# A gated recurrence and an FFT convolution in one kernel: the hidden state kept in natural order, and its transposes as float32r matmuls on an identity

## The chip, the cores and the metric

One core of a Trainium2 chip runs the whole program. The metric is device time in microseconds (us). TensorE is written PE (its weight loads PEld), VectorE is DVE, ScalarE is ACT, GpSimd is POOL, SyncE is SP; SP issues all DMAs of this kernel. SBUF is the on-chip memory with 128 partitions, PSUM the eight banks (512 float32 per partition each) that PE writes.

## The reference, cut to what matters

```
# x, f_logit: [4, 6272, 256] float32; lower_bound: [256]
f = lower_bound + (1 - lower_bound) * sigmoid(f_logit)
i = 1 - f
for t in range(6272):                      # for each batch and channel
    h = f[:, t] * h + i[:, t] * x[:, t]
    y[:, t] = h
proj = y @ w_proj                          # w_proj: [256, 768]
x1, x2, x3 = proj split in three
x2_conv = irfft(rfft(x2, time) * rfft(filter_fft, time))   # circular, length 6272
out = (x1 * x2_conv * x3) @ w_out          # [4, 6272, 256] float32
```

The length is 6272 = 128 x 49. The kernel computes the circular convolution as a two-dimensional transform over these factors, all as matmuls on small constant matrices.

## The kernel before, in words

Everything is done batch by batch (four batches, `b` = 0 to 3), and inside a batch in stages. Python generators hold the stages, and `weave` calls two of them alternately, so that their instructions are emitted in turn; a scheduler of the language then settles the order on each engine, and each engine works through its own list in order.

- `hgrn(b)` is the recurrence. It goes over time in 16 chunks of 392. SP loads a chunk of x (`xt`) and of f_logit (`ft`) with time on the partitions, 98 rows to a block. ACT takes the sigmoid, POOL multiplies (line 123), PE transposes both into PSUM (`sT` line 128, `uT` line 132) so that the channels lie on the partitions; ACT makes the gate `fT` (line 135), DVE runs the scan (line 138). The two halves of the channels (`kh` = 0, 1) do this one after the other. POOL then copies the scan's float32 result to float16 into `hG` (line 143), where times with the same remainder modulo 49 lie together.
- `phase_p(b)` projects h to x2. For each of 49 values of `q` POOL copies a rotated piece of `hG` into `hP` (lines 364 and 366), PE multiplies (line 368), ACT casts the result (line 370). `phase_f1(b)` is the first transform (PE line 382) and DVE and ACT in turn write its result `A` (lines 386, 388).
- `phase_z(b)` makes the gates x1 and x3 (16 matmuls of 512 columns for a group, line 406), ACT scales one (line 411), DVE multiplies the two into `z` (line 412).
- `units(b)` has 16 steps: PE transforms `A` (`px`, line 442), DVE multiplies by the filter's spectrum (lines 446 and 447), combines real and imaginary parts into `Y` (lines 450, 451), POOL adds a column (line 452), PE transforms back (`pi`, lines 457 and 459), ACT writes `Th` (line 463). `mini(b)` does the same for a special frequency.
- `phase_o(b)` finishes: PE (`pc`, line 478), DVE multiplies into `z` (line 482), PE multiplies by w_out (`po`, line 491), ACT scales (line 495), SP writes the output.
- `prepare` computes the constants and the filter's spectrum once: seven loads of 896 KB (line 287), a float32 matmul that rotates the rows (line 293), a split into two float16 parts (ACT line 297, DVE line 298), then 16 steps of transforms (lines 306 to 308 and 324).

The order of the stages is: `hgrn(0)` woven with `prepare`; then for each batch `phase_p` and `phase_f1` woven with `phase_z`, then `mini`, then `units` woven with the next batch's `hgrn`, then `phase_o`. PSUM tiles come from pools: two buffers for the transposes (`pst`), one for `px` (`psx`), two for all else (`psm`).

## Time and profile before

| what | value |
|---|---|
| two timed runs | 1226.43 and 1230.41 us, median 1228.42 us |
| the profiled execution | 1228.79 us; its span 1227.1 us; mean granted PE clock 0.803 |
| busy, share of the span | PE 73%, PEld 47%, DVE 52%, ACT 41%, POOL 32% |
| moved by DMA | 85.50 MB, mean 70 GB/s |

The span reaches from the first to the last instruction; what lies around it is 1.7 us. No engine is busy all the time, so the table alone does not name a bound: each stage has its own. The profile's groups give the mean time of one instruction and what ended the engine's waits; its windows give the busy time of each engine, and the clock that PE was granted, by stage.

### The profile page before, as it was taken

To read this page: it belongs to the slowest core of one execution; us is meant where nothing else is said; L and a number is where in the kernel's file an instruction comes from. 1 tells how busy PE (TensorE), PEld (TensorE's weight loads), DVE (VectorE), ACT (ScalarE), POOL (GpSimd) and SP (SyncE) were. 2 spreads that over 40 slices of the span, in tenths; PEclk is the share of its full clock that TensorE was granted. 3 is DMA by queue.
4 is the path that set the end of the run, shared out by engine and by line. 5 is a ranking of instruction groups with operands and counts; after the bars stand their busy time and mean duration, and the time that the engine had idled before them with its cause. 6 is when DMAs were issued, how large, how long until landed. Compare 5 with 4: busy or idle time off the path is not lost.

```text
span 1227.1 us, 14846 instructions
## 1 busy us (share of the span) xinstructions
PE 892.4 (73%) x5784; PEld 577.3 (47%) x5784; DVE 639.7 (52%) x806; ACT 504.3 (41%) x649; POOL 386.8 (32%) x701
## 2 busy tenths in 40 slices
PE   2676789886678848776778677867788568767765
PEld 1444566443355536543455455434455454333344
DVE  7766743123579834223779632235898322346632
ACT  5676754463233324543333324633333226321122
POOL 5433441450136593000346761001465800000000
PEclk9996599999955569999755579998655799995579
DMA  6344411000023425100233334000233130000013
GB/s 199 97 124 122 122 56 51 28 1 1 2 78 105 114 78 190 65 1 1 53 82 111 97 123 168 1 1 26 68 106 91 52 141 19 1 1 0 1 69 142
DMA packets 61350, 85.50 MB, mean 70 GB/s; under 512 B 3040, under 2 KB 53984, under 8 KB 61280
## 3 DMA queue, kind: packets, MB, share of 16 engines
q1 hardware_dynamic: 61280, 84.55, 21.9%
q8 instruction: 45, 0.74, 0.3%
q14 instruction: 25, 0.20, 0.1%
HBM read 58.85 MB, written 25.69 MB: 69 GB/s over the span
## 4 chain that ended last, share of the span: by engine, by line
PE 46%; DVE 28%; POOL 9%; ACT 8%; issue 7%; DMA 3%; POOLq 0%; SPq 0%; DVEq 0%; ACTq 0%
PE p L406 15%; PE po L491 8%; PE px L442 5%; DVE z L482 4%; DVE p L446 4%; DVE z L412 4%; DVE Y L451 4%; ACT x1s L411 4%; PE pfx L324 3%; PE pr L293 3%; DVE A L386 3%; DVE h L138 3%; POOL hP L366 3%; POOL xt L123 3%; PE pc L478 2%
## 5 line engine op out<-in xcount | busy, mean ns | idle before, releaser
L143 POOL CAST hG<-h 128x392 f16<-128x392 f32 x128 | 109.6, 861 | 359.9 <-PE p L406 262.2
L406 PE MATMUL p<-hG,W13h 128*128 128x512 f16 (+1 forms) x416 | 150.3, 368 | 83.2 <-DVE z L412 42.5
L123 POOL TENSOR_TENSOR xt<-xt,ft 98x1024 f32<-98x1024 f32 x64 | 157.4, 2461 | 131.5 <-DMA xt<-in_x_dram 54.9
L412 DVE TENSOR_TENSOR z<-p,x1s 128x512 f16<-128x512 f32 (+1 forms) x104 | 68.4, 658 | 182.4 <-ACT x1s L411 182.4
L463 ACT CAST Th<-pi 128x784 f16<-128x784 f32 x64 | 52.0, 812 | 245.9 <-PE pi L459 245.9
L406 PE MATMUL p<-hG,W13l 128*128 128x512 f16 (+1 forms) x416 | 150.3, 367 | 0.0
L132 PE MATMUL uT<-iden,xt 98*128 98x98 f32 x512 | 107.2, 353 | 53.5 <-ACT fT L135 27.9
L482 DVE TENSOR_TENSOR z<-pc,z 128x1024 f16<-128x1024 f32 (+1 forms) x52 | 60.5, 1163 | 153.7 <-PE pc L478 153.7
L491 PE MATMUL po<-Woh,z 128*128 128x256 f16 x392 | 99.3, 294 | 55.1 <-DVE z L482 53.2
L442 PE MATMUL px<-A,FT 98*128 98x512 f16 x256 | 118.9, 593 | 27.0 <-DVE p L447 20.4
L411 ACT ACTIVATE x1s<-p 128x512 f32<-128x512 f32 (+1 forms) x104 | 59.5, 572 | 169.1 <-PE p L406 168.6
L138 DVE TENSOR_TENSOR_SCAN h<-fT,h,uT 128x392 f32<-128x392 f32 x120 | 120.6, 1024 | 11.2 <-PE uT L132 7.1
L132 PEld LDWEIGHTS uT<-iden,xt 98*128 98x128 f32 x512 | 80.0, 206 | 85.1 <-ACT fT L135 43.5
L128 PE MATMUL sT<-iden,ft 98*128 98x98 f32 x512 | 105.3, 352 | 19.4 <-ACT ft L122 16.0
L457 PE MATMUL pi<-VA,Y 98*128 98x196 f16 x256 | 84.4, 364 | 43.9 <-POOL Y L452 43.9
L491 PEld LDWEIGHTS <-z 128*128 128x128 f16 x784 | 77.9, 105 | 77.1 <-DVE z L482 62.2
L446 DVE TENSOR_TENSOR p<-px,H 98x1024 f16<-98x1024 f32 x64 | 78.2, 1222 | 64.0 <-PE px L442 64.0
L128 PEld LDWEIGHTS sT<-iden,ft 98*128 98x128 f32 x512 | 83.2, 210 | 45.2 <-issue 14.9
L495 ACT ACTIVATE osb<-po 128x1024 f32<-128x1024 f32 (+1 forms) x52 | 50.6, 974 | 129.0 <-PE po L491 122.4
L406 PEld LDWEIGHTS <-W13l 128*128 128x128 f16 x416 | 40.5, 97 | 131.5 <-issue 97.1
L135 ACT ACTIVATE fT<-sT,nomc 128x392 f32<-128x392 f32 x128 | 77.4, 605 | 53.7 <-PE sT L128 51.4
L491 PE MATMUL po<-Wol,z 128*128 128x256 f16 x392 | 98.6, 292 | 0.0
(129 smaller groups left out, 1522.4 us busy)
## 6 DMA issues: line engine op xcount, KB each, us to landing
xt<-in_x_dram SPq DMA_DIRECT2D x64, 392.0 KB
ft<-in_f_logit_dram SPq DMA_DIRECT2D x64, 392.0 KB
out_dram<-osb SPq DMA_DIRECT2D x48, 512.0 KB
fraw<-in_moe_filter_fft_dram SPq DMA_DIRECT2D x7, 896.0 KB
wp<-in_moe_w_proj_dram SPq DMA_DIRECT2D x1, 768.0 KB
out_dram<-osb SPq DMA_DIRECT2D x4, 128.0 KB
wo<-in_moe_w_out_dram SPq DMA_DIRECT2D x1, 256.0 KB
wcol<-in_lower_bound_dram SPq DMA_DIRECT2D x1, 1.0 KB
```

The costliest lines, as they stand in the source:

```text
L123: nc.gpsimd.tensor_tensor(xt[:TB], xt[:TB], ft[:TB], op=AOP.mult)
L128: nc.tensor.transpose(sT[:, j * TB:(j + 1) * TB], ft[:TB, j, cols], iden[:TB, :TB])
L132: nc.tensor.transpose(uT[:, j * TB:(j + 1) * TB], xt[:TB, j, cols], iden[:TB, :TB])
L138: nc.vector.tensor_tensor_scan(h32[:], fT[:], uT[:, 0:CH], 0.0 if last[kh] is None else last[kh][:, CH - 1:CH], op0=AOP.mult, op1=AOP.add)
L143: nc.gpsimd.tensor_copy(hG[b][:, kh, :, c * MR:(c + 1) * MR], h32[:].rearrange("p (m r) -> p r m", r=Q))
L406: nc.tensor.matmul(p13[:, i, 0:cn], w[:, kh, js], hG[b][:, kh, r0:r0 + rn, :], start=(n == 0), stop=(n == 3))
L411: nc.scalar.activation(x1s[:, 0:cn], p13[:, 0, 0:cn], AF.Copy, scale=ZS)
L412: nc.vector.tensor_tensor(z[:, jb, r0:r0 + rn, :], p13[:, 1, 0:cn], x1s[:, 0:cn], op=AOP.mult)
L442: nc.tensor.matmul(px[:, o, :], FT[:TB, tb, :], A[:TB, es, r, :], start=(n == 0), stop=(n == 1))
L446: nc.vector.tensor_tensor(p0[:TB], px[:TB], H[:TB, :, u, :], op=AOP.mult)
L482: nc.vector.tensor_tensor(zz, pc[:, :, 0:rn * 128].rearrange("p a (i m) -> p a i m", m=128), zz, op=AOP.mult)
L491: nc.tensor.matmul(po[:, i, :], z[:, kh, r0 + i, :], w[:, kh, :], start=(n == 0), stop=(n == 3))
```

## The change

The hidden state is kept in the order of time, in float16, in one long tile `HA`: half 0 at the start, half 1 at the end, and between them the room of 16384 columns that holds `A`. The scan writes straight into it. What `phase_p` needs from `h` modulo 49 is read by PE with a step of 49 columns as the stationary operand; because such a read runs over the end of time, six DMAs (`wraps`) copy each half once more into the room of `A`, after `A` has been used. `phase_z` reads 490 consecutive columns (10 groups of 49) as its moving operand, and its DVE multiply brings the result into the old order of `z`, reading with a step of 49. The chunks of the recurrence have 512 times (13 chunks), on all 128 partitions. Sigmoid and product are written as float32r, and the transposes are ordinary matmuls of these with a float32r identity. In `units` the products of real and imaginary parts are no longer added by DVE: four products (`PP`) go to PE, which adds them (four matmuls where two stood; `VN` is minus `VA`). The filter is loaded row by row in rotated order, so that the rotation by PE goes. PSUM is one tile with banks chosen by hand: `pair()` goes round in four pairs of banks, `units` always uses banks 0 to 3, `phase_z` 4 and 5, `hgrn` 6 and 7.

The order of the stages: `phase_p` and `phase_f1` run alone, and `phase_z` is moved into `units`: each of 16 steps emits a step of `phase_z` (13 of them), one of `units` and, from the third step on, a chunk of the next `hgrn`.

```
+    HA = konst.tile([128, 2 * S + EW], F16, name="HA")
+    A = HA[:, S:S + EW].rearrange("m (e r k) -> m e r k", r=2, k=64)
+    HB = (0, S + EW)
...
+    PS = psp.tile([128, 8, 512], F32, name="PS")
...
     def hgrn(b):
...
-            nc.scalar.activation(ft[:TB], ft[:TB], AF.Sigmoid, scale=-1.0)
-            nc.gpsimd.tensor_tensor(xt[:TB], xt[:TB], ft[:TB], op=AOP.mult)
+            sr = hg.tile([128, 4, D], F32R, name="sr", tag="sr")
+            nc.scalar.activation(sr[:, 0:nb], ft[:, 0:nb], AF.Sigmoid, scale=-1.0)
+            ur = hg.tile([128, 4, D], F32R, name="ur", tag="ur")
+            nc.gpsimd.tensor_tensor(ur[:, 0:nb], xt[:, 0:nb], sr[:, 0:nb], op=AOP.mult)
             for kh in range(2):
...
-                    nc.tensor.transpose(sT[:, j * TB:(j + 1) * TB], ft[:TB, j, cols],
-                                        iden[:TB, :TB])
+                    nc.tensor.matmul(sT[:, j * 128:(j + 1) * 128], sr[:, j, cols], iden[:],
+                                     start=True, stop=True)
...
+                nc.vector.tensor_tensor_scan(
+                    HA[:, h0:h0 + n], fT[:, 0:n], uT,
+                    0.0 if c == 0 else HA[:, h0 - 1:h0], op0=AOP.mult, op1=AOP.add)
...
-                nc.gpsimd.tensor_copy(
-                    hG[b][:, kh, :, c * MR:(c + 1) * MR],
-                    h32[:].rearrange("p (m r) -> p r m", r=Q))
...
+    def wraps():
+        for a, z in ((0, 2048), (2048, 4096), (4096, E0)):
+            nc.sync.dma_start(HA[:, S + a:S + z], HA[:, a:z])
+        for a, z in ((128, 2048), (2048, 4096), (4096, S)):
+            nc.sync.dma_start(HA[:, HB[1] - S + a:HB[1] - S + z], HA[:, HB[1] + a:HB[1] + z])
...
     def prepare(tmp):
...
-            nc.sync.dma_start(raw, ff[:, r0:r0 + 7, :])
-            for r in range(r0, r0 + 7):
...
-                nc.tensor.matmul(pr[:, 0, 0:256], rot[:, m0_of(q):m0_of(q) + 128],
-                                 raw[:, r - r0, :], start=True, stop=True)
-                for p in range(2):
...
+            for q in range(q0, q0 + 7):
+                mm = -((128 * q - S) // Q)
+                nc.sync.dma_start(raw[0:mm, q - q0, :],
+                                  moe_filter_fft[128 * q:128 * q + Q * (mm - 1) + 1:Q, :])
+                if mm < 128:
+                    s0 = 128 * q + Q * mm - S
+                    nc.sync.dma_start(raw[mm:128, q - q0, :],
+                                      moe_filter_fft[s0:s0 + Q * (127 - mm) + 1:Q, :])
+            for p in range(2):
+                for e in range(2):
+                    c0 = p * 128 + e * 64
+                    src = raw[:, :, c0:c0 + 64].rearrange("m q g -> m g q")
+                    dh, dl = vh[:, p, e, :, q0:q0 + 7], vl[:, p, e, :, q0:q0 + 7]
+                    nc.scalar.copy(dh, src)
+                    nc.vector.tensor_tensor(dl, src, dh, op=AOP.subtract)
...
     def phase_p(b):
...
-                nc.gpsimd.tensor_copy(hP[:, :, q, 0:128 - m0], hG[b][:, :, r, m0:128])
-                if m0:
-                    nc.gpsimd.tensor_copy(hP[:, :, q, 128 - m0:128], hG[b][:, :, r, 0:m0])
                 for kh in range(2):
+                    n0 = HB[kh] + 128 * q - (S if kh and q else 0)
+                    nc.tensor.matmul(pp[:, q - q0, :], HA[:, n0:n0 + Q * 127 + 1:Q],
+                                     W2[:, kh, :], start=(kh == 0), stop=(kh == 1))
...
     def phase_z(b):
...
+                nc.vector.tensor_tensor(
+                    z[:, jb, :, m0:m0 + mn],
+                    PS[:, 5, 0:cn].rearrange("p (m r) -> p r m", r=Q),
+                    x1s[:, 0:cn].rearrange("p (m r) -> p r m", r=Q), op=AOP.mult)
...
     def units(b):
...
+            P = PP[:, u % 2]
+            nc.gpsimd.tensor_copy(P[:TB, 0, :, :, 0], zm[:TB, :, es])
...
+                nc.vector.tensor_tensor(P[:TB, o, :, :, 1:64],
+                                        px.unsqueeze(1).broadcast_to([TB, 2, UE, 63]), hh,
+                                        op=AOP.mult)
...
-            nc.vector.tensor_tensor(yf[:TB, 0], p0[:TB, 0], p0[:TB, 1], op=AOP.subtract)
-            nc.vector.tensor_tensor(yf[:TB, 1], p1[:TB, 0], p1[:TB, 1], op=AOP.add)
...
+                for n, (a, h, v) in enumerate(((0, 0, VA), (0, 1, VB), (1, 0, VB),
+                                               (1, 1, VN))):
+                    nc.tensor.matmul(o, P[:TB, a, h, 2 * pr:2 * pr + 2, :], v[:TB],
+                                     start=(n == 0), stop=(n == 3))
...
     for b in range(B):
-        weave((seq(phase_p(b), phase_f1(b)), 13 + NU), (phase_z(b), 26))
         mini(b)
-        if b + 1 < B:
-            weave((units(b), NU), (hgrn(b + 1), NCHK))
-        else:
-            run(units(b))
+        gu, gz = units(b), phase_z(b)
+        gh = hgrn(b + 1) if b + 1 < B else iter(())
+        for step in range(NU):
+            next(gz, None)
+            next(gu)
+            if step >= 2:
+                next(gh, None)
+        for g in (gu, gz, gh):
+            run(g)
+        if b + 1 < B:
+            wraps()
         run(phase_o(b))
+        if b + 1 < B:
+            run(phase_p(b + 1))
+            run(phase_f1(b + 1))
```

Three places show what this makes of the engines' lists. Line numbers of the rows after the change are those of the changed kernel, and in brackets stands the engine whose signal an instruction waits for.

The first is PE's list in the middle of `units(0)`. Before, a step has the four `px`, the eight back transforms that wait for POOL and DVE, and transposes of the next recurrence:

```order
L442 MATMUL px<-A,FT 128x512
L457 LDWEIGHTS Y [waits Pool_49]
L457 MATMUL pi<-VA,Y 128x196
L459 LDWEIGHTS Y [waits DVE_49]
L459 MATMUL pi<-VB,Y 128x196
...
L132 MATMUL uT<-iden,xt 128x98 [waits Activation_49]
L132 MATMUL uT<-iden,xt 128x98 x3
L128 MATMUL sT<-iden,ft 128x98 [waits DVE_49]
L128 MATMUL sT<-iden,ft 128x98 x3
```

After, line 421 is `phase_z`, 462 is `px`, 151 and 154 are the transposes of the sigmoid and the product, 474 the back transforms (16 in a step):

```order
L421 MATMUL PS<-HA,W13l 128x490
L462 LDWEIGHTS FT
L462 MATMUL PS<-HA,FT 128x512
...
L151 MATMUL PS<-iden,sr 128x128 x4
L154 MATMUL PS<-iden,ur 128x128 [waits Pool_49]
L474 LDWEIGHTS PP [waits DVE_49]
L474 MATMUL PS<-VA,PP 128x196
...
L154 MATMUL PS<-iden,ur 128x128 x3
L151 MATMUL PS<-iden,sr 128x128 [waits Activation_49]
```

The 16 matmuls of `phase_z` now stand ahead of each step's `px`, and the second half's transposes stand behind back transforms that wait for DVE.

The second is DVE's list at the same place. Before, a step has two products, two combinations and two scans:

```order
L446 TENSOR_TENSOR p_3280<-px,H 98x1024 [waits PE_49]
L447 TENSOR_TENSOR p_3281<-px,H 98x1024
L450 TENSOR_TENSOR Y<-p_3280 98x512 [waits DVE_49,Pool_49]
L451 TENSOR_TENSOR Y<-p_3281 98x512 [waits DVE_49]
L138 SCALAR_TENSOR_TENSOR h_3316<-fT,h_3257,uT 128x392 [waits PE_49,Activation_49,Pool_49]
L138 SCALAR_TENSOR_TENSOR h_3331<-fT,h_3272,uT 128x392 [waits PE_49,Activation_49,Pool_49]
```

After, two multiplies of `phase_z` (line 427), two products (466), two scans (160):

```order
L427 TENSOR_TENSOR z<-PS,x1s 128x49x10 [waits PE_49,Activation_49] x2
L466 TENSOR_TENSOR PP<-PS,H 98x16x63 [waits PE_49] x2
L160 SCALAR_TENSOR_TENSOR HA<-fT,HA,PS 128x512 [waits PE_49,Activation_49] x2
```

The combinations are gone, and the multiplies of `phase_z` stand ahead of the products. (DVE's rows by line 138 and 160 are the scans.)

The third is SP's list at the start, while the filter is loaded. Before, a load of the filter has 1792 elements on each of 128 partitions:

```order
L259 DMA wo<-in_moe_w_out_dram 128x2x256
L287 DMA fraw<-in_moe_filter_fft_dram 128x1792
L118 DMA xt<-in_x_dram 98x4x256
L120 DMA ft<-in_f_logit_dram 98x4x256
L287 DMA fraw<-in_moe_filter_fft_dram 128x1792 [waits DMAHW0_49]
```

After, a load is one row of 256 elements for each partition, in two pieces for most q:

```order
L317 DMA HA<-in_moe_filter_fft_dram 31x256 [waits DMAHW7_49]
L313 DMA HA<-in_moe_filter_fft_dram 95x256 [waits DMAHW0_49]
L317 DMA HA<-in_moe_filter_fft_dram 33x256 [waits DMAHW1_49]
L313 DMA HA<-in_moe_filter_fft_dram 92x256 [waits DMAHW2_49,DVE_49]
L317 DMA HA<-in_moe_filter_fft_dram 36x256 [waits DMAHW3_49]
...
L138 DMA xt<-in_x_dram 128x4x256 [waits DMAHW0_49,Pool_49]
```

Each waits for the DMA eight places ahead of it, some for DVE to have used the buffer, and the loads of x and f_logit stand between them in the same list. There are 97 such loads.

More of the change, by code (lines that the diff above doesn't have):

```diff
@@ L10 @@
 F32 = mybir.dt.float32
+F32R = mybir.dt.float32r
 F16 = mybir.dt.float16
@@ L136, in hgrn @@
+                for j in range(nb):
+                    nc.tensor.matmul(uT[:, j * 128:(j + 1) * 128], ur[:, j, cols], iden[:],
+                                     start=True, stop=True)
+                fT = hg.tile([128, CH], F32, name="fT", tag="fT")
+                nc.scalar.activation(fT[:, 0:n], sT, AF.Identity,
                                      scale=nomc[:, kh:kh + 1], bias=1.0)
-                h32 = hg.tile([128, CH], F32, name="h32", tag="h32", bufs=4)
+                h0 = HB[kh] + t0
@@ L389, in phase_f1 @@
             yield
-    def groups():
-        return [(r0, min(4, Q - r0)) for r0 in range(0, Q, 4)]
     def phase_z(b):
@@ L396, in phase_z @@
         st["z"] = z
-        for r0, rn in groups():
-            cn = rn * 128
+        for g in range(NZ):
+            m0 = g * ZR
+            mn = min(ZR, 128 - m0)
+            cn = mn * Q
             for jb in range(2):
-                p13 = psm.tile([128, 2, 512], F32, name="p13", tag="m")
                 for i in range(2):
@@ L468, in phase_o @@
         tf = Th[:].rearrange("p c g -> p (c g)")
-        for r0, rn in groups():
-            pc = psm.tile([128, 2, 512], F32, name="pc", tag="m")
+        for r0 in range(0, Q, 4):
+            rn = min(4, Q - r0)
+            pc = pair()
             for i in range(rn):
```

206 lines of the change are left out of this document (90 added, 116 removed).

## The prediction

> **What bounds the kernel now.** I read the clock row of the page first, then busy time by stage.
>
> ```profile
> PEclk9996599999955569999755579998655799995579
> ```
>
> The clock that PE is granted falls to half five times, once briefly in setup. The windows, cut where the work changes, say which stage it is (after start:end come the length, then busy us and instructions of PE, PEld, DVE, ACT, POOL, then clock, DMA share, GB/s):
>
> ```profile
> 30.00:160.00 130.00, 89.55 (x332) 62.71 (x333) 92.14 (x132) 91.70 (x140) 57.24 (x42) 0.80 0.40 116
> 160.00:240.00 80.00, 72.35 (x621) 46.82 (x619) 24.43 (x22) 39.14 (x44) 20.99 (x41) 0.98 0.14 41
> 240.00:336.00 96.00, 70.82 (x452) 39.33 (x452) 31.41 (x43) 42.44 (x56) 28.00 (x104) 0.97 0.00 1
> 336.00:461.00 125.00, 92.24 (x474) 63.02 (x475) 92.53 (x92) 41.80 (x57) 79.54 (x152) 0.55 0.31 93
> 461.00:505.00 44.00, 35.12 (x377) 26.59 (x376) 15.85 (x16) 18.61 (x22) 8.41 (x4) 0.94 0.51 178
> 1098.00:1174.00 76.00, 52.85 (x204) 26.58 (x205) 50.56 (x69) 13.71 (x18) 4.05 (x16) 0.52 0.00 1
> 1174.00:1227.00 53.00, 32.59 (x392) 24.67 (x392) 15.12 (x13) 12.66 (x13) 0.00 (x0) 0.95 0.30 122
> ```
>
> Setup takes 240 us. Batch 0 then takes 96 for projections, first transform and gates, 125 for `units` with the next recurrence, 44 for `phase_o`: 265. The last batch has `units` alone (76) and a full `phase_o` (53). `units` is where no engine is full and PE is at half speed: a chain from engine to engine. At its end the timeline shows one more loss:
>
> ```profile
> 692.99 8.51 POOL L366 COPY hP<-hG 128x4 f16<-128x4 f16 x38
> 701.75 0.35 PE L457 MATMUL pi<-VA,Y 98*128 98x196 f16 x1 [5.29 <-POOL Y L452]
> ```
>
> POOL copies pieces for the next `phase_p` ahead of the small copy that the last step waits for.
>
> **The change part by part.** I build the time from new stages, since almost every one is different. Durations of one instruction, from the groups:
>
> ```profile
> L138 DVE TENSOR_TENSOR_SCAN h<-fT,h,uT 128x392 f32<-128x392 f32 x120 | 120.6, 1024 | 11.2 <-PE uT L132 7.1 <-ACT f2h L297 4.1
> L446 DVE TENSOR_TENSOR p<-px,H 98x1024 f16<-98x1024 f32 x64 | 78.2, 1222 | 64.0 <-PE px L442 64.0
> L297 ACT CAST f2h<-pr 128x128 f16<-128x128 f32 x98 | 68.0, 766 | 36.0 <-PE pr L293 25.1 <-DVE f2l L298 8.5
> L370 ACT CAST x<-pp 128x1024 f16<-128x1024 f32 x48 | 67.8, 1412 | 14.3 <-PE pp L368 14.3
> L451 DVE TENSOR_TENSOR Y<-p 98x512 f16<-98x512 f16 x64 | 67.6, 1056 | 0.0
> L298 DVE TENSOR_TENSOR f2l<-pr,f2h 128x128 f16<-128x128 f32 x98 | 67.3, 745 | 26.8 <-ACT f2h L297 24.8
> L412 DVE TENSOR_TENSOR z<-p,x1s 128x512 f16<-128x512 f32 x96 | 66.1, 689 | 178.3 <-ACT x1s L411 178.3
> L411 ACT ACTIVATE x1s<-p 128x512 f32<-128x512 f32 x96 | 57.3, 597 | 166.6 <-PE p L406 166.6
> L386 DVE CAST A<-pa 98x1024 f16<-98x1024 f32 x32 | 39.1, 1223 | 63.3 <-PE pa L382 63.3
> L412 DVE TENSOR_TENSOR z<-p,x1s 128x128 f16<-128x128 f32 x8 | 2.3, 286 | 4.0 <-ACT x1s L411 4.0
> ```
>
> and starts of matmuls in the timeline (first number the start; an "x4" row runs from the first start to the last end):
>
> ```profile
> 139.81 0.67 PE L293 MATMUL pr<-fraw,rot 128*128 128x256 f32 x2 [1.05 <-issue]
> 157.90 0.22 PE L307 MATMUL pfa<-D,f2l 128*98 128x128 f16 x1
> 157.96 0.22 PE L308 MATMUL pfa<-D1l,f2h 128*98 128x128 f16 x1
> 250.19 0.38 PE L406 MATMUL p<-hG,W13l 128*128 128x512 f16 x1
> 250.41 0.38 PE L406 MATMUL p<-hG,W13h 128*128 128x512 f16 x1
> 473.59 0.56 PE L132 MATMUL uT<-iden,xt 98*128 98x98 f32 x4
> 1111.61 0.37 PE L459 MATMUL pi<-VB,Y 98*128 98x196 f16 x1
> 1111.77 0.37 PE L457 MATMUL pi<-VA,Y 98*128 98x196 f16 x1
> ```
>
> At full clock float16 starts every 0.055 us for 128 columns and 0.215 for 512; the back transforms stand 0.165 apart at half clock, so 0.083 at full.
>
> *The transposes, c each.* The trace has no float32r. Nearest: the old float32 transposes, four in 0.56 us, which less a pipeline of about 0.17 is 0.097 each for 98 columns, so 0.127 for 128. Lower end: float16, 0.055. Upper end: the ordinary float32 matmul, which the trace records as two instructions (98 for 49 calls); two take 0.67, less 0.17 and halved 0.25 for 256 columns, so 2 x 0.125 = 0.25 for 128. I take c = 0.127, the row for the same work. The Trainium skill, page "TensorE: Matmul & The Clock Gate", section Terms, says that trn2's loads and matmuls have a transpose mode four times as fast for float32, which would speak against giving it up. The trace agrees in direction, with a factor of 2: 0.99 us per thousand columns for the old transpose, 1.95 for the ordinary float32 matmul. What that would cost is the rival of slow transposes below.
>
> *The gate multiply, Z each.* It now reads with a step of 49. Without a penalty 490 columns cost 0.67 (of 0.689 for 512). For a step through SBUF there is one pair of PE rows, with and without it, in the answers for their lines:
>
> ```profile
> L421 PE MATMUL pm<-A,FT x8: 588/598/607, 329.6 to 1098.9; 98*128 98x256 f16 x8
> ```
> ```profile
> L335 PE MATMUL pfm<-mX,FT x4: 273/273/283, 239.1 to 239.6; 98*128 98x256 f16 x4
> ```
>
> 325 ns more over 256 columns is 1.27 more each, 1.69 in all. DVE's own rate is (689 - 286)/384 = 1.05; at 1.69 instead, 490 cost 0.83 plus 0.15 fixed, Z = 1.0, which I take. The upper end is the filter's split on DVE: 745 against 286 for the same 128 columns, 3.6 ns more each, which gives Z = 2.4.
>
> *A step of `units`, with gates and recurrence.* PE's list gives the order. Half a gate step (8 x 0.215 = 1.7, then 0.2 until DVE starts at 1.9), multiply Z, the waiting quarter (0.1 + 0.82), 0.2, second multiply Z: the two products start at 3.0 + 2Z and take 2 x 1.22. The back transforms stood behind them: 0.1 + 0.17 for the first group, 3c for transposes, 0.2, then the scan (1024 ns for 392, so 1.27 for 512) and, waiting for it, four more transposes: 5.5 + 2Z + 0.5 + 3c + 1.3 + 4c = 7.3 + 2Z + 7c, 10.2 us; I add 0.1 for DVE's second scan, which still runs when the next multiply is due. The removed combination (L451, 1.06, its wait for POOL behind it) is already out of it. PE's own work in the step is 3.4 + 0.9 + 16 x 0.083 + 16 x 0.127 = 7.7, 75% of 10.3. Which clock that gets I read from other stages. The last `phase_o` (53 us, clock 0.95) has only these on PE in a group, by the chain of waits:
>
> ```profile
> 1200.72 1.92 PE po L491 x16
> 1202.64 0.57 PE pc L478 x16
> 1204.52 1.92 PE po L491 x16
> ```
>
> Less the pipeline's 0.17 each, 1.75 + 0.4 = 2.15 of 3.8 us, 57%. The 125-us stage has, at full clock's prices, 4 x 0.215 + 8 x 0.083 + 16 x 0.097 = 3.1 in some 6.2 a step (97 us before POOL's copies, 16 steps), 50%, at 0.55. So 75% should keep the full clock.
>
> The stage: 11 full steps 113, two without recurrence (8.8 each) 18, two without gates (5.8 each) 12, one bare 4, and 3 for `mini`: 150. In the last batch there is no recurrence: PE's work is 5.7, the chain 8.8; the gates' matmuls stand between the back transforms there, so I take 7 x 13 + 3 x 4.4 = 104 and 3 for `mini`.
>
> *`phase_p` and `phase_f1` alone.* 98 matmuls with a strided stationary operand: at 1.69 x 128 = 0.21 each 21 us, near ACT's 13 casts at 1.41 + 0.04 = 19. The transform: DVE and ACT with eight evictions each, 1.22, so 10, and 2 for ends: 33. If a strided load costs nothing, ACT still holds it at 31. POOL's copies (L366) go; nothing takes their place.
>
> *`phase_o`.* Unchanged, 49 (53 in the last batch, as now). The wraps, 3.1 MB a batch, mostly start when pieces of `A` are used up, and `phase_o` hides the rest; if that cover is gone, they cost the output's stall, up to 8 us a batch.
>
> *Setup.* The rotations (L293) and 98 + 98 narrow splits go; 28 + 28 wider ones come, bounded by 448 elements at 0.55 (no penalty) and 2.2 us (3.6 ns more each), under the loads as I see it. What is late then is the loading. Rows of SP's timeline and of the page:
>
> ```profile
> 3.28 0.46 SPq L287 DMA_DIRECT2D fraw<-in_moe_filter_fft_dram  x1
> ```
> ```profile
> GB/s 199 97 124 122 122 56 51 28 1 1 2 78 105 114 78 190 65 1 1 53 82 111 97 123 168 1 1 26 68 106 91 52 141 19 1 1 0 1 69 142
> ```
>
> 97 loads at 0.46 are 45 us on SP; the bytes up to there (filter and weights 7.4 MB, five chunks 5.2 MB) take 64 us at 199 GB/s and 103 at 122. I take 85. Then 16 filter steps: 24 x 0.055 + 12 x 0.215 = 3.9 of PE each, and between each two a chunk, 16c + 1.4 of waits for the gate and the scan: 8 x (7.8 + 3.4) = 90, against 80 now. The last wraps are exposed once: about 8. `phase_p` and `phase_f1` of batch 0: 33.
>
> *Sum:* 85 + 90 + 8 + 33 + 3 x (150 + 49 + 33) + 107 + 53 = 1072, and the 1.7 us that the profiled execution (1228.79) has around its span of 1227.1: 1074. That execution is 0.4 above the median of the two runs, 1228.42, so nothing is corrected: 1075 us, 12.5% less.
>
> **The rivals.** *Both unknowns are cheap* (Z = 0.67, c = 0.055): a full step is 1.2 shorter, 33 of them 40 us; the last batch 9; transposes in setup 13 x 16 x 0.072 = 15; loads at full rate 20: 1075 - 84 = 991. For it: the page's first slice of 199 GB/s.
>
> *Slow transposes* (c = 0.25): PE's own list becomes the longer chain, 6.8 + 2Z + 11c, so 1.25 more in 33 steps, 0.9 in six others, and 13 x 16 x 0.123 = 26 in setup: 1075 + 72 = 1147. For it: the ordinary float32 matmul is two records. Against it: the changed program has one matmul for one transpose.
>
> *The loading of the filter is the bound*: eight loads in flight, each small, and x and f_logit behind them. At 97 GB/s, the page's second slice, 12.6 MB take 130: 1075 + 45 = 1120.
>
> *Dear strides* (Z = 2.4): 2.8 more in 4 x 13 steps, 146: 1221, no change that shows.
>
> *PE stays at half clock* in the merged stage, which ends on the other side. Place: the middle of each step, where PE waits for the products 1.2 us and for the scan. The price: a step is then PE's 15.4 us, 5.1 more in 33, 168; the last batch's 11.4 instead of 7, 57; the short steps 20: 1320 us, slower. It decides when PE's share falls to between 50 and 57%: at a step of some 14 us, to which a dear stride (13.1) comes near. For it: the windows' 0.52 in the stage of `units` alone, whose matmuls at full clock would be 1.5 us of every 4.3. Against it: the 75% above. [...]
>
> ```profile
> 1109.76 1.89 PE L442 MATMUL px<-A,FT 98*128 98x512 f16 x4 [1.14 <-DVE p L447]
> 1114.10 1.89 PE L442 MATMUL px<-A,FT 98*128 98x512 f16 x4 [1.14 <-DVE p L447]
> ```
>
> **How the numbers follow.** Chances: the forecast 0.46, cheap unknowns 0.16, slow transposes 0.13, slow loading 0.08, dear strides 0.09, half clock 0.08. The forecast's own range is 1035 to 1115. From 985 to 1180 the first four cases lie inside, 0.83. A difference under 2% is about what a measurement of this kernel can't tell from none. Faster by more than that: the first four, 0.83; within: dear strides 0.09; slower: half clock 0.08.
>
> **What would show it.** Right: merged stage near 150 us at a clock over 0.9, gate multiplies near 1.0 us, transposes 0.13 apart, setup ready for `phase_p` near 183 us, no POOL copies ahead of `phase_o`. Each step is wrong if its own figure is off. I am wrong as a whole if the clock in the merged stage is near 0.5, if the multiplies take over 2 us, or if a PSUM bank that `hgrn` and `pair()` share in setup makes the filter's steps wait for the scan far longer than the 1.4 us I allow.

## The result and the profile after

The changed kernel takes 1018.62 us (median of two runs, 1015.33 to 1021.9), against 1228.42 before: a ratio of 0.829, 95% interval 0.824 to 0.834, 17.1% less. The forecast was 1075 (12.5% less). The direction was right, and the time lies in the range of 985 to 1180, but below the forecast's own range of 1035 to 1115. The sum does not hold term by term: setup took 49 us more than forecast and the rest 101 less, so part of the agreement is luck. And the part that gives the change its name, the float32r matmuls, cost time. One execution of all, in e11, took 2485 us, nearly three times as long as its others; nothing here explains it, and the ratio given there leaves it out.

The clock row of the page of the kernel after, first. It no longer shows the five long falls to half:

```profile
PEclk9999998987979897899898978998988989899999
```

The windows of the kernel after, cut at its own stages (columns as in the prediction): loading, filter steps with the last recurrence chunks, `phase_p` and `phase_f1` of batch 0, merged stage, `phase_o`, then the last batch's units with gates and its `phase_o`:

```profile
0.00:120.60 120.60, 17.06 (x64) 14.63 (x64) 55.83 (x135) 42.16 (x52) 16.07 (x28) 1.00 0.38 113
120.60:232.10 111.50, 96.55 (x715) 69.39 (x715) 43.22 (x38) 54.39 (x66) 28.66 (x43) 0.92 0.38 113
232.10:264.20 32.10, 23.67 (x227) 21.18 (x227) 8.71 (x9) 25.42 (x28) 2.34 (x1) 0.79 0.16 51
264.20:408.60 144.40, 124.31 (x728) 81.17 (x729) 94.80 (x90) 55.97 (x82) 32.97 (x29) 0.88 0.34 108
408.60:444.50 35.90, 31.06 (x388) 25.54 (x389) 14.14 (x12) 11.33 (x12) 0.00 (x0) 0.91 0.40 160
888.50:979.90 91.40, 83.39 (x532) 46.10 (x533) 64.11 (x63) 27.75 (x43) 3.98 (x16) 1.00 0.00 1
979.90:1019.90 40.00, 30.50 (x392) 24.91 (x392) 14.56 (x13) 12.68 (x13) 0.00 (x0) 0.95 0.40 162
```

What each term of the sum came to. Where a term stands for several batches, the others are read between the same marks, the first matmuls of the stages in the timeline (the merged stages of batches 1 and 2 begin with gates' matmuls at 473.3 and 681.1):

| term | forecast | after | difference |
|---|---|---|---|
| loading, to the first filter step | 85 | 120.6 | +35.6 |
| filter steps and exposed wraps | 98 | 111.5 | +13.5 |
| `phase_p`, `phase_f1`, four batches | 132 | 118.6 | -13.4 |
| merged stage, three batches | 450 | 431.6 | -18.4 |
| `phase_o`, four batches | 200 | 146.2 | -53.8 |
| units and gates of the last batch | 107 | 91.4 | -15.6 |
| sum | 1072 | 1019.9 | -52.1 |

No run takes back the merged stage, the order of the hidden state or the four products by itself, so how the 17.1% divide among the parts of the change is not shown.

From the groups of the kernel after, the prices that the forecast had to estimate (mean ns behind the bar):

```profile
L427 DVE TENSOR_TENSOR z<-PS,x1s 128x490 f16<-128x490 f32 x96 | 95.3, 993 | 84.8 <-PE PS L421 76.4 <-ACT Th L477 3.1 <-ACT x1s L426 2.5
L387 ACT CAST x<-PS 128x1024 f16<-128x1024 f32 x48 | 62.5, 1501 | 5.2 <-PE PS L385 5.2
L324 ACT CAST f2h<-HA 128x448 f16<-128x448 f32 x28 | 25.0, 961 | 51.1 <-DMA ft<-in_f_logit_dram 26.2 <-DMA HA<-in_moe_filter_fft_dram 24.9
```

And from its timeline: three groups of transposes in setup; three ends of a step of the merged stage and two of the last batch (ACT's cast to `Th`, once a step); PE's wait for the product in such a step; gates' matmuls inside and behind a stretch at half clock; three rows of `phase_o`:

```profile
138.37 0.61 PE L154 MATMUL PS<-iden,ur 128*128 128x128 f32 x4
139.82 0.66 PE L151 MATMUL PS<-iden,sr 128*128 128x128 f32 x4 [0.85 <-ACT fT L157]
141.14 0.66 PE L154 MATMUL PS<-iden,ur 128*128 128x128 f32 x4 [0.58 <-DVE HA L160]
...
318.49 0.81 ACT L477 CAST Th<-PS 128x784 f16<-128x784 f32 x1 [2.63 <-PE PS L474]
328.00 0.81 ACT L477 CAST Th<-PS 128x784 f16<-128x784 f32 x1 [2.63 <-PE PS L474]
338.23 0.81 ACT L477 CAST Th<-PS 128x784 f16<-128x784 f32 x1 [3.34 <-PE PS L474]
...
946.65 0.81 ACT L477 CAST Th<-PS 128x784 f16<-128x784 f32 x1 [2.29 <-PE PS L474]
952.66 0.81 ACT L477 CAST Th<-PS 128x784 f16<-128x784 f32 x1 [2.29 <-PE PS L474]
...
306.64 0.26 PE L474 MATMUL PS<-VA,PP 98*128 98x196 f16 x1 [0.89 <-DVE PP L466]
...
300.40 0.61 PE L421 MATMUL PS<-HA,W13h 128*128 128x490 f16 x1
302.66 0.37 PE L421 MATMUL PS<-HA,W13h 128*128 128x490 f16 x1
...
422.09 1.08 PE L494 MATMUL PS<-ID,Th 64*128 64x128 f16 x32
424.04 0.28 PE L506 MATMUL PS<-Woh,z 128*128 128x256 f16 x1 [0.87 <-DVE z L498]
427.64 1.08 PE L494 MATMUL PS<-ID,Th 64*128 64x128 f16 x32
```

Four transposes behind a wait take 0.66 us: less the pipeline of 0.17, 0.122 each. Right behind four others they take 0.61, or 0.11 each. A step with recurrence takes 9.51 us where PE keeps its clock (318.49 to 328.00) and up to 11.4 where it does not. From 295.7 to 302.4 us, 6.7 us, PE is at half clock (the gates' matmuls stand 0.41 apart instead of 0.21); such stretches come five times in this stage, each about one, two or three times 3.4 us long, and make the mean clock 0.88. The last batch has no transposes, a clock of 1.00 and steps of 6.01 us. In `phase_o` 32 matmuls of `pc` (line 494) stand together, two groups at once, and two groups take 5.55 us: 2.77 each, not the 3.8 of before.

### The profile page after: what moved, and what is told of

It is laid out like the page before. It is cut to its first block, busy times and chain, and to the rows that moved or that the text cites. A ratio compares the mean times of both kernels' runs of the same rounds, so it can differ in the third digit from the quotient of the medians.

```text
span 1019.9 us, 14543 instructions
## 1 busy us (share of the span) xinstructions
PE 780.6 (77%) x5958; PEld 555.6 (54%) x5958; DVE 538.9 (53%) x586; ACT 436.6 (43%) x541; POOL 145.2 (14%) x173
## 4 chain that ended last, share of the span: by engine, by line
PE 42%; DVE 23%; issue 14%; ACT 11%; DMA 6%; SPq 3%; POOL 1%; DVEq 0%; ACTq 0%; POOLq 0%
PE PS L421 11%; DVE PP L466 10%; PE PS L474 9%; PE PS L506 7%; DVE z L427 6%; ACT x L387 5%; DMA HA<-in_moe_filter_fft_dram 4%; PE PS L350 4%; DVE z L498 2%; ACT fT L157 2%; PE PS L154 2%; PE PS L397 2%; DVE HA L160 2%; PE PS L462 1%; ACT x1s L426 1%
## 5 line engine op out<-in xcount | busy, mean ns | idle before, releaser
L160 DVE TENSOR_TENSOR_SCAN HA<-fT,HA,PS 128x512 f16<-128x512 f32 (+1 forms) x96 | 116.2, 1210 | 120.5 <-ACT fT L157 70.6
L421 PE MATMUL PS<-HA,W13h 128*128 128x490 f16 (+1 forms) x416 | 165.4, 398 | 13.0 <-ACT x1s L426 8.8
L421 PE MATMUL PS<-HA,W13l 128*128 128x490 f16 (+1 forms) x416 | 163.5, 393 | 0.0
L427 DVE TENSOR_TENSOR z<-PS,x1s 128x490 f16<-128x490 f32 (+1 forms) x104 | 101.8, 979 | 93.5 <-PE PS L421 83.2
L466 DVE TENSOR_TENSOR PP<-PS,H 98x1008 f16<-98x1008 f32 x128 | 149.0, 1199 | 3.2 <-PE PS L462 3.1
L145 POOL TENSOR_TENSOR ur<-xt,sr 128x1024 fp32r<-128x1024 f32 (+1 forms) x52 | 116.6, 2243 | 214.3 <-ACT sr L143 164.2
L474 PEld LDWEIGHTS <-PP 98*128 98x128 f16 x1024 | 90.7, 106 | 79.7 <-DVE PP L466 53.7
L474 PE MATMUL PS<-VB,PP 98*128 98x196 f16 x512 | 105.8, 269 | 10.4 <-DVE PP L466 9.6
L506 PE MATMUL PS<-Woh,z 128*128 128x256 f16 x392 | 93.2, 284 | 20.4 <-DVE z L498 20.4
L506 PE MATMUL PS<-Wol,z 128*128 128x256 f16 x392 | 92.7, 283 | 0.0
```

Source lines behind the costliest of these rows:

```text
L145: nc.gpsimd.tensor_tensor(ur[:, 0:nb], xt[:, 0:nb], sr[:, 0:nb], op=AOP.mult)
L160: nc.vector.tensor_tensor_scan(HA[:, h0:h0 + n], fT[:, 0:n], uT, 0.0 if c == 0 else HA[:, h0 - 1:h0], op0=AOP.mult, op1=AOP.add)
L421: nc.tensor.matmul(PS[:, 4 + i, 0:cn], w[:, kh, js], HA[:, h0:h0 + cn], start=(n == 0), stop=(n == 3))
L427: nc.vector.tensor_tensor(z[:, jb, :, m0:m0 + mn], PS[:, 5, 0:cn].rearrange("p (m r) -> p r m", r=Q), x1s[:, 0:cn].rearrange("p (m r) -> p ...
L466: nc.vector.tensor_tensor(P[:TB, o, :, :, 1:64], px.unsqueeze(1).broadcast_to([TB, 2, UE, 63]), hh, op=AOP.mult)
L474: nc.tensor.matmul(o, P[:TB, a, h, 2 * pr:2 * pr + 2, :], v[:TB], start=(n == 0), stop=(n == 3))
```

## The experiments

Each run is compared with the kernel before, on the same chip; the kernel after stands at 0.829 on that scale.

**e1: the order of `phase_o`.** `pc` gets one fixed pair of banks:

```
-            pc = pair()
+            pc = PS[:, 0:2]
...
-            po = pair().rearrange(...)
+            po = PS[:, 2 + r0 % 8 // 2:4 + r0 % 8 // 2].rearrange(...)
```

> phase_o with one fixed pair of banks for pc and two in turn for po, so that PE again goes pc, po, pc, po; nothing else differs from the changed kernel. Theory (the four pairs that pair() hands out let PE do two groups of pc ahead of two of po, and this alone shortened phase_o from 3.8 to 2.8 us a group): a group takes 3.7 to 3.9 us again, phase_o 47 to 50 us, the whole 4 x 12 = 48 us more than 1019: 1060 to 1075. Rival (phase_o is shorter for another reason, such as the clock or fewer transfers beside it): a group stays at 2.7 to 2.9 us and the whole at 1012 to 1028.

1056.61 us, ratio 0.861 (0.857 to 0.865): 38 more than the kernel after, a little under what the theory asked. Its timeline of `phase_o`:

```profile
423.20 0.62 PE L494 MATMUL PS<-ID,Th 64*128 64x128 f16 x16
425.15 0.28 PE L506 MATMUL PS<-Woh,z 128*128 128x256 f16 x1 [1.32 <-DVE z L498]
427.00 0.62 PE L494 MATMUL PS<-ID,Th 64*128 64x128 f16 x16
```

A group is back at 3.80 us, and PE waits 1.32 us for `z` in each. The stage takes 47 us again. So the shorter `phase_o` comes from the pairs of banks: with four pairs in turn the scheduler puts two groups of `pc` together and PE waits 0.87 once for two groups.

**e2: the transposes back to float32.**

```
-            sr = hg.tile([128, 4, D], F32R, ...)      (ur alike)
+            sr = hg.tile([128, 4, D], F32, ...)
-                    nc.tensor.matmul(sT[...], sr[:, j, cols], iden[:], start=True, stop=True)
+                    nc.tensor.transpose(sT[...], sr[:, j, cols], iden32[:])   (uT alike)
```

> The one part of the change that its name speaks of is undone: s and u are float32 tiles again and are transposed by TensorE's transpose with the float32 identity, 512 columns at a time as in the changed kernel. Theory (a float32r matmul on an identity costs what the old transpose cost, 0.123 us now against 0.127 scaled from the old one): four in 0.66 to 0.70 us and 1012 to 1028 us in all. Rival A (the float32r form is what made the merged stage fit): transposes of 0.25 us, 1070 to 1110. Rival B (the float32r matmuls are what lowers the clock in the stages with recurrence, 0.88 against 1.00 without): the clock of the merged stage rises over 0.95, each stage is 8 to 12 us shorter, 985 to 1000.

932.87 us, ratio 0.759 (0.756 to 0.761): 86 less than the kernel after, more than any theory gave. Its windows (batch 0's merged stage) and its timeline:

```profile
251.10:371.00 119.90, 107.34 (x728) 68.29 (x729) 93.06 (x90) 55.44 (x82) 32.98 (x29) 1.00 0.39 125
```

```profile
298.02 0.66 PE L153 MATMUL PS<-iden,ur 128*128 128x128 f32 x4
...
302.68 0.60 PE L151 MATMUL PS<-iden,sr 128*128 128x128 f32 x4
303.12 0.60 PE L153 MATMUL PS<-iden,ur 128*128 128x128 f32 x4
303.56 0.37 PE L419 MATMUL PS<-HA,W13h 128*128 128x490 f16 x1
304.26 0.26 PE L472 MATMUL PS<-VA,PP 98*128 98x196 f16 x1 [0.33 <-DVE PP L464]
...
306.77 0.80 ACT L475 CAST Th<-PS 128x784 f16<-128x784 f32 x1
315.34 0.80 ACT L475 CAST Th<-PS 128x784 f16<-128x784 f32 x1
```

The clock is 1.00, as Rival B says, but a step is 8.57 us, 0.94 shorter than the float32r kernel's at full clock too. The price of a transpose doesn't explain that: four float32 ones take 0.66 or 0.60 by their place, four float32r ones 0.66 or 0.61. The rows show something else: the scheduler has given PE another order. Both first groups of transposes and a gate matmul stand ahead of the back transforms, and PE waits 0.33 for the product there, against 0.9 in the kernel after. Two things changed with one edit; e5 and e6 part them.

**e5 and e6: form and order apart.** Each kernel gets the other's order of instructions, by edges that force an order and wait for nothing:

```
+    for steps in table.values():          # one list of instructions for PE, DVE, ACT, POOL
+        ...
+            tc.add_manual_dep(ins, prev.name, DependencyInfo(NoSync, DATA))
```

> The changed kernel with its float32r matmuls, but PE, DVE, ACT and POOL are made to issue in exactly the order that the scheduler chose for the kernel with float32 transposes (e2): a table of that order, kept by ordering edges without a wait. The two kernels differ then in the form of the transposes alone. Theory (the order is what cost the 86 us: in it gates' matmuls stand on PE while DVE makes the products, so that the step is shorter and the clock stays up): 935 to 960 us, clock over 0.96, transposes still 0.122 apart. Rival (the float32r matmul itself lowers the clock or is slower): 990 to 1020 us at a clock near 0.92.

> The other half: float32 transposes in exactly the order that the scheduler chose for the changed kernel with float32r. Theory (the order cost the 86 us): 990 to 1020 us, clock near 0.92, transposes 0.108 apart, a step with recurrence still over 9.2 us. Rival (the form of the transposes cost them): 930 to 950 us at a clock near 0.98.

| | order of the kernel after | order of e2 |
|---|---|---|
| float32r | 1018.62, ratio 0.829 (0.824 to 0.834) | e5: 943.59, 0.766 (0.763 to 0.770) |
| float32 | e6: 984.88, 0.803 (0.799 to 0.807) | e2: 932.87, 0.759 (0.756 to 0.761) |

By the tiles that they read, PE's 5958 recorded matmuls stand in one order in the kernel after and e6, and in another in e2 and e5. The order is worth 75 us with float32r and 52 with float32; the form is worth 34 in the one order and 11 in the other. The theory of the order holds for most of the 86. The merged stage of batch 0 in e5's windows, then in e6's:

```profile
253.80:374.50 120.70, 108.22 (x726) 71.14 (x725) 92.87 (x89) 55.54 (x82) 32.97 (x29) 0.98 0.40 126
```
```profile
257.30:391.80 134.50, 112.04 (x728) 69.72 (x729) 94.71 (x90) 55.38 (x82) 32.97 (x29) 0.97 0.36 119
```

and a step in the timelines of the two:

```profile
309.38 0.80 ACT L498 CAST Th<-PS 128x784 f16<-128x784 f32 x1
317.95 0.81 ACT L498 CAST Th<-PS 128x784 f16<-128x784 f32 x1
```
```profile
307.37 0.81 ACT L495 CAST Th<-PS 128x784 f16<-128x784 f32 x1 [2.58 <-PE PS L492]
316.86 0.81 ACT L495 CAST Th<-PS 128x784 f16<-128x784 f32 x1 [2.58 <-PE PS L492]
```

At full clock a step takes 8.57 us in the one order and 9.49 in the other, whatever the form: 9.51 and 9.49, 8.57 and 8.57. So the form costs a step nothing directly; its share shows in the clock, 0.88 against 0.97 in the order of the kernel after.

**e12: float16 transposes in the order of the kernel after**, by the same kind of table.

```
-            sr = hg.tile([128, 4, D], F32R, ...)      (ur and iden alike)
+            sr = hg.tile([128, 4, D], F16, ...)
```

> The changed kernel in its own order on PE, DVE, ACT (a table, as in e6; on POOL two copies change places), but s, u and the identity are float16 in the transposes, which leaves out their lower bits: a transpose of 128 columns should stand 0.055 apart instead of 0.122, and PE has 16 x 0.067 = 1.1 us less to do in a step of 9.5. It asks why float32r has a clock of 0.88 in this order where float32 has 0.97. Theory (something in the float32r matmul itself lowers the clock): clock of the merged stage 0.95 or more, a step 9.5 us or less, 970 to 985. Rival (the clock falls when PE is busy for too little of the time): with still less to do the clock is under 0.90, and the whole over 1000.

1007.29 us, ratio 0.818 (0.816 to 0.821). Its windows, batch 0's merged stage:

```profile
261.50:404.90 143.40, 117.50 (x726) 71.27 (x725) 94.50 (x89) 55.90 (x82) 30.18 (x29) 0.85 0.35 112
```

The clock is as low without float32r, so the theory that float32r itself lowers it falls. But PE's work doesn't put the three forms in order either: float16, at 0.055 a transpose the least, has 0.85; float32r and float32, both at about 0.11, have 0.88 and 0.97.

A count from the traces narrows it. Their record of the clock changes only at the ends of pieces of 3.41 us. Take for each piece the columns of the matmuls that start in it, at 0.42 ns a column (512 take 0.215 us at full clock), as a share of the piece. In the three merged stages of the kernel after, the 18 pieces at full clock that a fall follows have shares of 0.23 to 0.46, and of the 77 others all but one have 0.49 or more. In e12 it is 0.20 to 0.48 for the 28 before a fall, and 0.49 or more for 56 of the 61 others. In e6 only three pieces come before a fall, with 0.27 to 0.35, and 16 of 0.48 or less keep the clock. So the falls go with the work in one piece of 3.41 us and not with that of a whole step, and a float32 transpose seems to count for more than its columns. No run tests this by itself, and why float32 should count for more stays open.

**e3: the step of 49 in the gate's multiply.**

```
-                    z[:, jb, :, m0:m0 + mn],
-                    PS[:, 5, 0:cn].rearrange("p (m r) -> p r m", r=Q),
-                    x1s[:, 0:cn].rearrange("p (m r) -> p r m", r=Q), op=AOP.mult)
+                    z[:, jb].rearrange("p r m -> p (r m)")[:, m0 * Q:m0 * Q + cn],
+                    PS[:, 5, 0:cn], x1s[:, 0:cn], op=AOP.mult)
```

> The gate's multiply reads and writes 490 columns in order, with no step of 49; this leaves out the reordering of z, so that phase_o meets the gates in the wrong order. Theory of the prediction (a multiply stands twice in the chain of every step with recurrence): each takes 0.65 to 0.70 us instead of 0.99, a full step 0.65 us less, 33 steps 21 us: 993 to 1003. Rival (PE's own work, slowed by stretches at half clock, bounds the step and the multiply is covered): multiplies just as short, but 1012 to 1024 in all.

972.63 us, ratio 0.792 (0.789 to 0.795): 46 less, twice what the theory gave. The multiply's group, batch 0's merged stage in the windows, and a step:

```profile
L427 DVE TENSOR_TENSOR z<-PS,x1s 128x490 f16<-128x490 f32 x96 | 64.2, 668 | 77.7 <-PE PS L421 66.8 <-ACT Th L476 4.1 <-ACT x1s L426 3.0
```
```profile
265.70:394.10 128.40, 111.94 (x728) 74.45 (x725) 86.55 (x90) 55.43 (x82) 32.88 (x29) 0.96 0.37 122
```
```profile
303.69 0.81 ACT L476 CAST Th<-PS 128x784 f16<-128x784 f32 x1 [2.30 <-PE PS L473]
312.65 0.81 ACT L476 CAST Th<-PS 128x784 f16<-128x784 f32 x1 [2.30 <-PE PS L473]
```

The step at full clock falls by 0.55 us, close to the 0.65 of two multiplies, and PE's order is that of the kernel after: two multiplies stand in the chain of a step, as forecast. Eleven such steps are 6 us of the 16 that the stage loses. The clock, 0.96 instead of 0.88, accompanies the rest: it seems that here too a shorter wait in the step pays a second time through the clock.

**e4, e8, e9: the loading, with e7 for `phase_o`.** In e4 a load takes seven rows that lie side by side for each partition:

```
-                nc.sync.dma_start(raw[0:mm, q - q0, :], ...)          (97 of both kinds)
-                    nc.sync.dma_start(raw[mm:128, q - q0, :], ...)
+            nc.sync.dma_start(raw[:], moe_filter_fft.rearrange("(a r) d -> a r d", r=Q)[:, q0:q0 + 7, :])
```

> The 97 filter loads become seven of 896 KB, each of seven rows side by side for every partition; this leaves out the order of the filter's rows. Same bytes. Theory (setup is bound by the number of small loads, about 1.1 us each with the waits on SP): the first filter step starts at 65 to 80 us instead of 120.6, and the whole is 40 to 55 us less than 1019: 962 to 982. Rival (the bytes, or the chunks that share the queue, are the bound): it starts after 105 us and the whole is 1000 to 1022.

970.42 us, ratio 0.790 (0.786 to 0.795), first filter step at 61.2. The figure is the theory's, but the edit changed the count of loads, the length of their rows and the partitions of each, all at once. e7 and e8 stand on e2; e7 also writes `phase_o` ahead by hand:

```
+        for k in range(len(groups) + 1):
+            if k < len(groups):
+                front(*groups[k])          # pc of group k, its product z
+            if k:
+                back(*groups[k - 1])       # po of the group before, its store
```

> Float32 transposes as in e2, and phase_o written so that pc of the next group stands ahead of po of this one on PE, with two pairs of banks for each. Theory (PE waits 0.9 us for the product of z in every two groups, 5.55 us a pair; without that wait a group is 16 x 0.109 + 0.5 of PE): 2.2 to 2.4 us a group instead of 2.8, 6 us a batch, 900 to 915 in all. Rival (the output's stores or ACT's eviction take over as the bound): 2.6 to 2.8 a group and 925 to 937.

922.82 us, ratio 0.751 (0.749 to 0.753): 10 less than e2. Two starts in its `phase_o`:

```profile
384.94 0.62 PE L491 MATMUL PS<-ID,Th 64*128 64x128 f16 x16
387.34 0.62 PE L491 MATMUL PS<-ID,Th 64*128 64x128 f16 x16
```

A group takes 2.40 us and PE has no wait in it: the figure for a group holds, that for the whole does not. 13 x 0.37 is 4.8 a batch, not 6, and in e2 the stage of batch 0 was down to 33.5 us already. e8 cuts the count to 20 loads and keeps the rows of 1 KB:

```
+            for m0, m1, base, off in ((0, lo, moe_filter_fft, 0), (lo, hi, seam, SEAM0),
+                                      (hi, 128, moe_filter_fft, S)):
+                ...one load of partitions m0 to m1 with seven rows each
```

> As e7, and the filter's rows in their right order by 20 loads instead of 97: the rows on both sides of the wrap are copied once into a scratch in DRAM, and each seven residues are one piece ahead of the wrap, one from the scratch and one behind the wrap. Theory (the count of loads is the bound of setup): first filter step at 62 to 78 us instead of 120, the whole 35 to 50 less than e7: 855 to 878. Rival (the copy into the scratch and its reading back cost what the count saves): under 15 us less than e7.

964.95 us, ratio 0.785 (0.783 to 0.787): 42 more than e7, and the first filter step at 163.4. With fewer loads the loading takes longer, so their count is not the bound. SP's timeline of e8, and two rows of the DMA view of its window from 14 to 30 us (GB/s in 40 slices; queue, packets, MB and share of 16 engines):

```profile
13.89 29.69 SPq L322 DMA_DIRECT2D HA<-seam  x1
```
```profile
GB/s 26 23 26 23 23 26 23 23 23 23 23 23 23 23 23 23 23 23 44 23 23 23 23 20 23 23 23 23 23 23 23 23 23 23 23 23 23 23 23 23
q1 hardware_dynamic: 362, 0.37, 6.8%
```

SP stands for 30 us, for 8.6 of them because of the copy into the scratch, while one load of 113 partitions and 791 KB moves at 23 GB/s with a share of 6.8%, about one of 16 engines. 113 is a prime number, and so are the 73 and 109 of the two other slow loads. The kernel after has such stretches too, in its DMA view from 99 to 105 us:

```profile
GB/s 27 21 20 27 20 20 27 20 27 20 20 27 20 20 27 20 20 27 20 20 27 20 27 20 20 27 20 20 27 20 20 27 20 21 27 20 20 27 20 21
q1 hardware_dynamic: 138, 0.14, 6.8%
```

Suppose that a load uses as many engines as the largest divisor up to 16 of its number of partitions, and that each moves 23 GB/s. By this estimate the 97 loads one after the other need 97 us, 59 of them in the 20 loads with one engine. SP needs 109 for them with the chunks between. The Trainium skill has this rule (page "DMA: Bandwidth & Descriptors", section "Why a DMA increments its semaphore by 16 and not by 1"): the engines of a transfer are the largest number up to 16 that divides the slowest dimension on both sides, and 127 partitions use one. The trace agrees with its 6.8%. e9 tests the estimate on the kernel after:

```
                 mm = -((128 * q - S) // Q)
+                s0 = 128 * q + Q * mm - S
+                mm = mm // 16 * 16
...
```

> The changed kernel with the split between the two filter loads of a residue moved down to the next multiple of 16 partitions: 91 loads instead of 97, the same bytes, each row still 1 KB. This gives up to 15 partitions a residue the wrong rows. Theory (a load is spread over as many of the 16 DMA engines as divide its number of partitions, so that the 20 loads with a prime number go through one engine at 23 GB/s, 59 us of the 97 us that all of them take one after the other; loads in e8 with 113, 73 and 109 partitions moved 23 GB/s for 34, 24 and 33 us): first filter step at 65 to 85 us instead of 120.6, whole 965 to 990. Rival (the count of loads is the bound, 1.1 us each, as e4 was meant to show): first step after 110, whole 1008 to 1024.

974.58 us, ratio 0.794 (0.791 to 0.796), 44 less, with 91 loads and rows as long as before. The first filter step in its timeline:

```profile
72.01 0.40 PE L335 MATMUL PS<-D,f2h 128*128 128x128 f16 x2 [4.24 <-ACT f2h L326]
```

The numbers of partitions explain 48.6 of the 59.4 us between the 120.6 of the kernel after and e4's 61.2; the rest goes to rows and count, which no run parts.

**e10 and e11: a faster kernel.** e10 is e8 with its cuts at multiples of 16:

```
-            lo = -((128 * (q0 + 6) - S) // Q)
-            hi = -((128 * q0 - S) // Q)
+            lo = -((128 * (q0 + 6) - S) // Q) // 16 * 16
+            hi = min(128, (15 - (128 * q0 - S) // Q) // 16 * 16)
```

> As e8 (float32 transposes, phase_o written ahead, 20 filter loads with a scratch in DRAM for the rows around the wrap), with the three pieces cut at multiples of 16 partitions; the scratch grows from 1.8 to 3.0 MB. Theory of the engines (as in e9): the loads' long single-engine stretches go, first filter step at 60 to 85 us, whole 865 to 890, 35 to 55 less than e7. Rival (the copy through the scratch is what made e8 slow): still over 930.

884.83 us, ratio 0.721 (0.718 to 0.723): 38 less than e7, first filter step at 79.3. The scratch, larger here than in e8, is thus not what made e8 slow. e11 adds:

```
-            nc.scalar.copy(xv[:, :, q0:q0 + qn], ...)
+            cast = nc.vector.tensor_copy if q0 % 8 else nc.scalar.copy
+            cast(xv[:, :, q0:q0 + qn], ...)
```

> As e10, and phase_p's casts alternate between ACT and DVE, which has nothing to do there. Theory (ACT's 13 casts of 1.5 us are the bound of phase_p, about 19 us, PE's own 98 matmuls about 13.5): phase_p 4 to 5 us shorter in each of four batches, 15 to 20 less than e10 in all. Rival (DVE's scattered write costs it so much, or PE's strided loads bind, that nothing is won): within 5 us of e10.

857.58 us, ratio 0.699 (0.697 to 0.700): 27 less than e10, 161 less than the kernel after. Its casts in the groups:

```profile
L394 ACT CAST x<-PS 128x1024 f16<-128x1024 f32 x24 | 34.4, 1450 | 10.7 <-PE PS L391 10.7
L394 DVE CAST x<-PS 128x1024 f16<-128x1024 f32 x24 | 34.4, 1442 | 27.1 <-PE PS L391 27.1
```

DVE's scattered write costs what ACT's does. `phase_p` and `phase_f1` of batch 0 take 25.7 us instead of 31.6, and in all four batches 28 less, more than the 15 to 20 of the theory: the first transform, which the edit doesn't touch, is 1.5 to 2 us shorter in each batch too, for a reason that no run shows.

## Why the prediction was right or wrong

The measured 1018.62 lies nearer to the 991 of the rival of cheap unknowns than to the 1075 of the forecast. But that rival's conditions all failed: Z is 0.99 and not 0.67, c is over 0.1 and not 0.055, and the loads were slow. The chain of the merged stage is the forecast's; the difference comes mostly from `phase_o` and the loading, two misses that partly offset each other:

- **Transposes, c = 0.127:** 0.122 behind a wait, by the same working, and 0.11 behind others. Right. The float32 transpose costs the same (0.66 or 0.60 for four). The Trainium skill's transpose mode that is four times as fast for float32 (page "TensorE: Matmul & The Clock Gate", section Terms) speaks against the change. e2 agrees in sign, with 86 us, but not by this mechanism: no row here shows the two forms a factor of four apart.
- **The gate's multiply, Z = 1.0:** 0.993. Right, with some luck: the price of the step came from rows of PE, and no run shows why DVE's should be the same.
- **A full step, 7.3 + 2Z + 7c:** 9.51 at full clock, 10.2 in the mean of the nine steps that end between 297.5 and 389.5 us, against 10.3 forecast. The mean is right for a mixed reason: the list's chain is 0.8 shorter than I made it, and stretches at half clock give that back. Of the chain's parts, e3 measured the two multiplies; the others were not measured one by one.
- **Clock over 0.9 in the merged stage:** wrong, 0.88. I took the share of PE's busy time as the rule, with a threshold between 50 and 57%. By the forecast's own measure, work at full clock's prices, it is some 7.5 of 10.2 us a step, over 70%, and 86% by the windows' busy time; the clock still falls for stretches of 3.4 us or a multiple. The mean of a step was the wrong measure: by the count under e12, the work in single pieces of 3.41 us falls under half. The rival of half clock was right about its place: PE's wait for the products, which e2 and e5 shorten from 0.9 to about 0.33. It was wrong about its size, 12% of the clock and not 50. The Trainium skill (page "TensorE: Matmul & The Clock Gate", section HAM oscillation) gives as the abstract rule "no PE-idle gaps >~3.4µs". Keeping to it is not enough here: the longest wait of PE in batch 0's stage is 1.00 us, and the clock falls.
- **The last batch, 7 a step:** 6.01. Mis-sized: I let the gates' matmuls delay the chain, and PE's own 5.7 us are nearly the bound. PE waits 0.25 a step for the products, and in e3, with the shorter multiply, a step takes 5.69.
- **`phase_p` and `phase_f1`, 33:** 32.1 in batch 0 and 28 to 29 in the others, with casts of 1.50. Nearly right, and held by ACT, as e11 shows. The strided stationary operand, for which I allowed 0.21 us a matmul, costs nothing that shows: in batch 1 PE does 51 of these matmuls in 5.91 us, or 0.11 each.
- **`phase_o`, "Unchanged, 49":** the worst step, 53.8 us in four batches. Its code is the same, its banks are not. I read PE's order for the merged stage only; in `phase_o` the same list shows two groups of `pc` together. e1 brings the old 3.80 back.
- **Loading, 85:** 120.6, the other large miss. I sized it by bytes and by SP's issue time, and left out how many engines a load uses; e9 shows the number of partitions as the cause of most of it. The rival of slow loading had 130, from a rate and not from this mechanism.
- **Filter steps:** the waits I allowed, 1.4 us a chunk, are 0.85 + 0.58 = 1.43. The 13.6 us of two steps and a chunk (139.82 to the same row at 153.41) exceed my 11.2; a stretch at half clock in it, 32 matmuls at 0.107 instead of 0.055, is 1.7 of the 2.4. In e2's order the whole piece takes 98, as the forecast's 90 and 8 for the wraps have it, but the wraps are not in it: PE waits for them only behind the first matmuls of `phase_p`.
- **The wraps, 8:** PE waits 2.6 us for them, inside the 32.1 of `phase_p` and `phase_f1` of batch 0.

## What to carry to other kernels

A change of an instruction's form can move the scheduler's whole order. Before crediting or blaming the form, pin the order and swap one at a time: here the order was worth 52 to 75 us and the form 11 to 34. Code that the diff doesn't touch is not unchanged when its buffers are: read the order there too. And look at the number of partitions of each load: here loads with a prime number of them kept about one of 16 DMA engines busy, and cutting at multiples of 16 took 48.6 us off the loading.

## What was not expected of the hardware

- A load of 113 partitions moved 23 GB/s with a share of 6.8% of the engines; moving cuts to multiples of 16 brought the first filter step from 120.6 to 72.0 us.
- At 86% busy by the windows PE still lost its clock, in stretches of about 3.4, 6.7 and 10 us. In one order of instructions the clock was 0.97 with float32 transposes, 0.88 with float32r and 0.85 with float16 ones; the count of columns in pieces of 3.41 us under e12 says when it fell, but not why float32 differs.
- In the first 120 us the clock's record says 1.00, but PE is nearly idle there and four transposes take 1.11 us, against the 0.66 at 139.82. From the timeline of the kernel after:

```profile
28.80 1.11 PE L151 MATMUL PS<-iden,sr 128*128 128x128 f32 x4 [13.49 <-ACT sr L143]
```

The clock row can't be read where PE hardly runs.
